# A fused retention-attention and MLP kernel: attention blocks in 64x64 quadrants without the masked quarter, swapped key halves, and a reordered lead-in

## The chip, the cores and the metric

The kernel runs on one core of a Trainium2 chip. The metric is the device time of one execution in microseconds; a kernel's time is the median of its runs. The span in a profile is some 1.8 us shorter than the time of the same execution. Ratios are the mean time of one kernel's fast runs over the mean of the other's fast runs of the same rounds, so not quite the ratio of the quoted medians.

Names used below: PE is TensorE, DVE VectorE, ACT ScalarE, POOL GpSimd, SP SyncE.

## The reference

```python
# q, k, v: (8 batches, 8 heads, 576 positions, 64), float32
scores = (1/8) * q @ k^T
rel    = pos[:, None] - pos[None, :]
ret    = scores * where(rel >= 0, gamma_h ** rel, 0)     # causal, with decay per head
x      = (ret @ v), laid out as (4608 tokens, 512)
h      = x @ w_in                                        # 512 x 2048
out    = (h * sigmoid(1.702 * h)) @ w_out                # 2048 x 512
```

## The kernel before

The tokens are cut into 36 units of 128; four units make a chunk, nine chunks make the run. For each chunk the kernel computes `up` (16 column blocks of 4 matmuls of 128x512, then Gelu on ACT) and `down` (4 row blocks of 16 matmuls). The attention of the next chunk's units is put between them in `block`, two units at a time: `inter` (contribution of the state of earlier units), `scores` (keys times queries of the following two units), a mask product on DVE, `values`. `state` updates a 64x64 key-value state per head. Keys and queries come as float32 over POOL's DMA queue, are cast to bf16 by it, and from unit 8 on are transposed by a DMA transpose from SP into `kqT`; the first eight units are transposed on PE.

```python
def load_kq(u, which, eng="pool"):          # one DMA for k, one for q (two each for a tail unit)
    ... e.dma_start(kqn[sl][p0:p0+n, which, :, :], src[b, :, s0:s0+n, :].rearrange("h p d -> p h d"))

def dma_transpose(u):                       # on SP, in order with the stores
    op("sp", lambda e: e.dma_start_transpose(kqT[u % NQT].ap(), kqn[sl]...), ...)

def scores(u, banks):                       # 8 matmuls in 64x128 shape
    for hp in range(HP):
        for hh in range(2):
            matmul(ps32(banks[hh])[:, P*hp : P*hp+P],
                   qt[64*hh : 64*hh+64, hp, :], qt[64*hh : 64*hh+64, HP+hp, :])

def values(u, slot):                        # 8 matmuls in 128x64 shape
    ... matmul(xbank(hh, slot)[64*pb : 64*pb+64, g, :], vp[u % NVP][:, 2*hp+hh, :], pm[u % 4][hh][:, hp, :])

def block(j):                               # inter is in 64x64 shape
    inter(2*j, 0); inter(2*j+1, 1)
    scores of units 2j+2, 2j+3
    values(2*j, 0); values(2*j+1, 1)
    ...

def lead_in():
    load_kq(0, 0); load_kq(0, 1); load_v(0); iota_small()
    load_v(1, after=["kq0_1"])              # v of units 0 to 3 from SP, each behind a landing
    load(1); iota_large(); load_win(0); ... load(2) ... load(3); weights
    for u in range(4, NLD): load(u)         # NLD = 12
    ... units 0 to 3, half-width ups, full ups, down of chunk 0 with units 4 to 7 ...

def steady():
    for c in range(1, NCH):
        for u in range(4*c+6 if c > 1 else NPE, min(4*c+10, NU)):
            dma_transpose(u)                # chunk 1: units 8 to 13, behind all stores of chunk 0
        for f in range(NF):
            up(c, f)
            if f % 4 == 2: state(m); load(m + NLD)
            ...
            if c == 1 and f == 8: scores(8, "CD"); scores(9, "EX")
```

## Time and profile before

The median on the first chip is 334.57 us (333.93 to 336.38).

| part of the run (PE timeline) | from, us | lasts, us |
|---|---|---|
| chunk 0 and everything ahead of it | 0 | 69.8 |
| chunk 1 | 69.8 | 44.7 |
| chunks 2 to 7, each | 114.5 | 31.1 to 31.6 |
| chunk 8 (no attention) | 303.0 | 30.5 |

From the page of before: the busy share of PE, the granted clock and the DMA in 40 slices of 8.3 us, in tenths, and the chain of waits by engine.

```profile
PE   6365999984499999999999999999999999999996
PEclk9557899998589999999999999999999999999999
DMA  9999999999999199339915992870170162011012
PE 83%; DMA 9%; ACT 3%; DVE 2%; issue 2%; SPq 1%; POOL 0%; POOLq 0%
```

PE is full except in the first four slices, in slices 9 to 11 and at the very end. The waits that the change goes after lie in the first two of these places; elsewhere only PE work can be saved. The second hole is this, in the chain in order of time (start, length, what):

```profile
71.11 1.54 SPq L342
72.76 15.07 DMA kqT<-kqn
```

and from PE's side (start, length, instructions, and in brackets the idle time before and what ended it):

```profile
76.98 1.03 PE L457 MATMUL psA<-xT,w_in_sb 128*128 128x512 bf16 x4
81.88 0.28 PE L404 MATMUL psC<-kqT 64*128 64x128 bf16 x1 [3.88 <-DMA kqT<-kqn]
87.89 0.28 PE L404 MATMUL psE<-kqT 64*128 64x128 bf16 x1 [5.40 <-DMA kqT<-kqn]
88.83 1.49 PE L457 MATMUL psB<-xT,w_in_sb 128*128 128x512 bf16 x3 [0.33 <-issue]
```

The transposes of units 8 and 9 are issued at 71.1 and 72.8 us, and the second lands 15 us after its issue. PE stands for most of 11 us, and its matmuls then run at half clock.

A steady block of two units looks like this in PE's timeline (lines left out between the ends of each group):

```profile
201.57 0.24 PE L392 MATMUL psX<-kqT,kv 64*64 64x128 bf16 x1
...
201.66 0.22 PE L392 MATMUL psY<-kqT,kv 64*64 64x128 bf16 x1
201.80 0.23 PE L404 MATMUL psB<-kqT 64*128 64x128 bf16 x1
...
202.21 0.22 PE L404 MATMUL psE<-kqT 64*128 64x128 bf16 x1
202.35 0.30 PE L423 MATMUL psX<-pm,vp 128*64 128x128 bf16 x4
...
202.71 0.28 PE L423 MATMUL psY<-pm,vp 128*64 128x128 bf16 x4
203.15 0.38 PE L468 MATMUL psA<-w_out_sb,gT 128*128 128x512 bf16 x1 [0.16 <-issue]
```

Starts tell more than lengths here, because matmuls overlap. Pairs of scores start 0.055 us apart; at each change of shape (64*64 to 64*128, to 128*64, to 128*128) the start is some 0.09 us later than that pace would give. One record is missing ahead of the last line, which is why 203.15 is 0.22 us late.

### The profile page before, as it was taken

How to read it: one execution, taken by the hardware profiler on the slowest of the kernel's cores; microseconds unless marked ns; L12 is line 12 of the kernel's file. 1: busy time of each engine (PE TensorE's matmuls, PEld its weight loads, DVE VectorE, ACT ScalarE, POOL GpSimd, SP SyncE). 2: the span in 40 equal slices, each digit the busy share in tenths (PEclk: the TensorE clock that was granted, in tenths of full speed). 3: DMA queues.
4: the chain of work that ended last, by engine and by line, in shares of the span. 5: the costliest groups of instructions: out<-in, count | busy, mean ns of one | idle time of the engine just before them, and what ended most of it. 6: DMA issues, size and time to landing. Idle time of an engine off the chain costs nothing.

```text
span 333.5 us, 5231 instructions
## 1 busy us (share of the span) xinstructions
PE 301.1 (90%) x2198; PEld 144.8 (43%) x2232; DVE 119.3 (36%) x224; ACT 127.9 (38%) x230; POOL 107.3 (32%) x136
## 2 busy tenths in 40 slices
PE   6365999984499999999999999999999999999996
PEld 2133634531154444443544444444445444443344
DVE  4325002861234435433551455324534434510000
ACT  5463653343041263136314611661164136314721
POOL 8996298962160068008303630400000000000000
PEclk9557899998589999999999999999999999999999
DMA  9999999999999199339915992870170162011012
GB/s 99 158 194 202 209 213 224 234 231 135 100 131 202 64 175 177 100 97 166 180 65 130 188 156 65 132 88 34 66 158 2 63 80 47 2 63 63 2 31 94
DMA packets 121063, 40.19 MB, mean 120 GB/s; under 512 B 110160, under 2 KB 114512, under 8 KB 121040
## 3 DMA queue, kind: packets, MB, share of 16 engines
q0 software_dynamic: 81920, 22.03, 63.4%
q1 hardware_dynamic: 39120, 17.83, 28.8%
q8 instruction: 17, 0.28, 0.3%
q14 instruction: 6, 0.05, 0.0%
HBM read 36.70 MB, written 9.44 MB: 138 GB/s over the span
## 4 chain that ended last, share of the span: by engine, by line
PE 83%; DMA 9%; ACT 3%; DVE 2%; issue 2%; SPq 1%; POOL 0%; POOLq 0%
PE psA L468 19%; PE psB L457 18%; PE psA L457 18%; PE psB L468 18%; DMA kqT<-kqn 5%; DMA vn<-in_v_dram 3%; PE psK L353 2%; PE psX L423 2%; DVE pm L412 1%; PE psY L423 1%; PE psX L392 1%; PE psB L404 1%; DMA kqn<-in_q_dram 1%; PE psD L404 1%; ACT kqT L325 1%
## 5 line engine op out<-in xcount | busy, mean ns | idle before, releaser
L457 PE MATMUL psA<-xT,w_in_sb 128*128 128x512 bf16 (+1 forms) x297 | 76.8, 379 | 3.2 <-ACT gT L462 2.8
L457 PE MATMUL psB<-xT,w_in_sb 128*128 128x512 bf16 (+1 forms) x296 | 76.0, 379 | 0.7 <-issue 0.3
L468 PE MATMUL psA<-w_out_sb,gT 128*128 128x512 bf16 (+1 forms) x288 | 66.7, 373 | 2.2 <-issue 2.1
L209 POOL DMA_DIRECT2D kqn<-in_k_dram x40 | 35.5, 899 | 101.5 <-PE psK L353 91.6
L468 PE MATMUL psB<-w_out_sb,gT 128*128 128x512 bf16 (+1 forms) x285 | 63.9, 373 | 0.3 <-issue 0.2
L462 ACT ACTIVATE gT<-psB 128x512 bf16<-128x512 f32 (+1 forms) x76 | 43.7, 574 | 37.4 <-PE psB L457 37.1
L462 ACT ACTIVATE gT<-psA 128x512 bf16<-128x512 f32 (+1 forms) x76 | 43.7, 574 | 21.8 <-PE psA L457 21.7
L366 DVE CAST kv<-psK 64x256 bf16<-64x256 f32 x56 | 23.6, 422 | 77.3 <-PE psK L353 76.9
L457 PEld LDWEIGHTS psA<-xT,w_in_sb 128*128 128x128 bf16 x304 | 27.0, 101 | 41.4 <-ACT gT L462 16.9
L468 PEld LDWEIGHTS psA<-w_out_sb,gT 128*128 128x128 bf16 x304 | 28.2, 98 | 31.4 <-ACT gT L462 1.0
L468 PEld LDWEIGHTS psB<-w_out_sb,gT 128*128 128x128 bf16 x288 | 27.9, 98 | 31.5
L457 PEld LDWEIGHTS psB<-xT,w_in_sb 128*128 128x128 bf16 x304 | 25.9, 101 | 31.5 <-ACT gT L462 10.5
L478 ACT ACTIVATE osb<-psA 128x512 f32<-128x512 f32 x18 | 10.7, 597 | 71.3 <-PE psA L468 71.3
L209 POOL DMA_DIRECT2D kqn<-in_q_dram x40 | 35.3, 889 | 2.6 <-issue 2.6
L222 POOL DMA_DIRECT2D vn<-in_v_dram x36 | 32.4, 909 | 4.6 <-issue 4.5
L307 DVE TENSOR_TENSOR vp<-vn,vfac 128x512 bf16<-128x512 f32 x36 | 24.6, 689 | 15.7 <-DMA vn<-in_v_dram 15.0
L478 ACT ACTIVATE osb<-psB 128x512 f32<-128x512 f32 (+1 forms) x18 | 10.5, 586 | 48.7 <-PE psB L468 48.7
L412 DVE TENSOR_TENSOR pm<-psC,mask 128x512 bf16<-128x512 f32 x20 | 13.7, 683 | 22.0 <-PE psD L404 22.0
L412 DVE TENSOR_TENSOR pm<-psB,mask 128x512 bf16<-128x512 f32 x12 | 8.3, 691 | 36.9 <-PE psB L404 36.9
L404 PE MATMUL psC<-kqT 64*128 64x128 bf16 x88 | 9.3, 230 | 8.1 <-ACT kqT L325 4.2
L423 PE MATMUL psX<-pm,vp 128*64 128x128 bf16 x144 | 10.1, 233 | 5.6 <-DVE pm L412 5.6
L353 PE MATMUL psK<-vp,kqn 128*128 128x128 bf16 x128 | 13.3, 231 | 0.0
(61 smaller groups left out, 195.6 us busy)
## 6 DMA issues: line engine op xcount, KB each, us to landing
out_dram<-osb SPq DMA_DIRECT2D x31, 256.0 KB, 2.1
vn<-in_v_dram POOLq DMA_DIRECT2D x28, 256.0 KB, 12.8
kqn<-in_k_dram POOLq DMA_DIRECT2D x32, 128.0 KB, 11.4
kqn<-in_q_dram POOLq DMA_DIRECT2D x32, 128.0 KB, 11.4
w_in_sb<-in_moe_w_in_dram POOLq DMA_DIRECT2D x8, 256.0 KB, 11.4
w_out_sb<-in_moe_w_out_dram POOLq DMA_DIRECT2D x4, 512.0 KB, 20.5
out_dram<-osb SPq DMA_DIRECT2D x10, 128.0 KB, 2.3
vn<-in_v_dram SPq DMA_DIRECT2D x4, 256.0 KB, 9.5
```

Of the source, the lines that this page charges most:

```text
L209: e.dma_start(kqn[sl][p0 : p0 + n, which, :, :], src[b, :, s0 : s0 + n, :].rearrange("h p d -> p h d"),)
L222: e.dma_start(vn[sl][p0 : p0 + n, :, :], v[b, :, s0 : s0 + n, :].rearrange("h p d -> p h d"),)
L307: op(eng, lambda e: e.tensor_tensor(vp[u % NVP].ap(), vn[sl].ap(), vfac[:, ty, :, None].to_broadcast([P, H, DH]), ALU.mult), reads=[f"vn{s ...
L353: op("pe", lambda e, hp=hp: e.matmul(bank["K"][:, P * hp : P * hp + P], kqn[sl][:, 0, 2 * hp : 2 * hp + 2, :], vp[u % NVP][:, 2 * hp : 2 * ...
L366: op("dve", lambda e, dst=dst, src=src: e.tensor_copy(dst, src), reads=["K"], writes=[f"kv{u % NKV}_{hh}"])
L404: op("pe", lambda e, hp=hp, hh=hh: e.matmul(ps32(banks[hh])[:, P * hp : P * hp + P], qt[64 * hh : 64 * hh + 64, hp, :], qt[64 * hh : 64 * ...
L412: op("dve", lambda e: e.tensor_tensor(pm[u % 4][hh].ap(), ps32(banks[hh]).rearrange("p (a i) -> p a i", i=P), m[:, None, :].to_broadcast([ ...
L423: op("pe", lambda e, g=g, pb=pb, hh=hh, hp=hp, s=s: e.matmul(xbank(hh, slot)[64 * pb : 64 * pb + 64, g, :], vp[u % NVP][:, 2 * hp + hh, :] ...
L457: op("pe", lambda e, a=a: e.matmul(bank[b][:, n0:n1], w_in_sb[:, a, P * f : P * f + P], xT[c % 2][:, a, n0:n1], start=(a == 0), stop=(a == ...
L462: op("act", lambda e: e.activation(gT[c % 2][:, f, n0:n1], bank[b][:, n0:n1], AF.Gelu_apprx_sigmoid), reads=[b], writes=[f"g{c % 2}_{f}_{j ...
L468: op("pe", lambda e, f=f: e.matmul(bank[b][:, 0 : n1 - n0], gT[c % 2][:, f, P * r : P * r + P], w_out_sb[:, f, n0:n1], start=(f == 0), sto ...
L478: op("act", lambda e: e.activation(dst, src, AF.Copy), reads=[b], writes=[f"osb{i}_{n0}"])
```

## The change

It has two intents. First, units 9 to 35 do all their attention in 64x64 shape, so that the shape never changes inside a block, and they don't compute the quarter of key-query pairs in which all keys lie after all queries. Without more, one half of the array would stream 128 columns per head and the other 64. So the loads of the odd heads put keys (and v) into the partitions with their halves of 64 swapped: then each quadrant has a full and a half product in turn. That needs eight DMAs per unit instead of three. The author did not want two row groups to write one PSUM bank at once, so the values come in two phases, and the second waits for the first. Second, the lead-in is reordered: v of units 1 to 3 goes to POOL's queue behind k and q, tables are made by cheaper instructions, units 2 and 3 are interleaved with half-width ups, four banks are used. Units 8 and 9 are transposed behind the second store of chunk 0, and loads from unit 10 on wait for a transpose.

```diff
+def head(u, pb, g, hh):
+    if u < NSW:                        # NSW = 9
+        return 4 * pb + 2 * g + hh
+    return 4 * pb + 2 * hh + g
...
+    todo = [(slice(0, 4), slice(0, H, 2), r) for r in unit_rows(u)]          # load_kq, u >= NSW
+    odd = halves(u, True) if which == 0 else unit_rows(u)
+    todo += [(slice(4, 8), slice(1, H, 2), r) for r in odd]
...
+QR = {(0, 0): (0, 0, P), (0, 1): (64, 128, 64), (1, 0): (64, 0, 64), (1, 1): (0, 64, P)}
...  scores
+for pb in range(2):
+    for g in range(2):
+        for c in (g, 1 - g):
+            q0, o0, n = QR[c, g]
+            for hh in range(2):
+                matmul(ps32(banks[hh])[64*c : 64*c+64, 192*pb+o0 : 192*pb+o0+n],
+                       qt[64*hh : 64*hh+64, 2*g+pb, 64*c : 64*c+64],
+                       qt[64*hh : 64*hh+64, HP+2*g+pb, q0 : q0+n])
...
+def values_half(u, slot, phase, after_ops=()):
+    for g, r in ((0, 0), (0, 1), (1, 1), (1, 0)):
+        hh = r ^ phase ...             # row group r writes bank hh
...  block
+    first = [values_half(u, sl, 0)]    # ahead of the next units' scores
     scores(u, b) ...
+    values_half(u, sl, 1, first)       # behind them
...  lead_in, steady
-load_v(1, after=["kq0_1"])             # on SP
+load(1)                                # k, q, v on POOL
-for u in range(4, NLD): load(u)
+for u in range(4, NPE + 2): load(u)    # to unit 9
+                if r == 1:             # in down of chunk 0
+                    dma_transpose(8)
+                    dma_transpose(9)
+                if c == 1:
+                    for u in range(10, 14):
+                        load(u, after=["T1_0"])          # T1 is unit 9's transpose here
+                for u in range(4 * c + 10, 4 * c + 14):
+                    load(u, after=[f"T{(4 * c + 9) % NQT}_0"])
```

## The prediction

> **What bounds it now.** The chain of waits puts 73% of the span on the dense up and down matmuls. In the timeline a chunk of four units (128 dense 128x512 matmuls and their attention) repeats every 31.4 to 31.5 us from 146 us on; four dense matmuls take 0.86 us, so 27.6 us is dense and 3.8 us attention. PE is full there at clock 1.0, so only PE time counts. The first two differ: chunk 0 ends at 69.8 us and chunk 1 takes 44.8 us.
>
> **Lead-in.** The chain waits 9.3 us for v of unit 1, whose load the sync queue issues only after unit 0's q landed: PE stands from 12.4 to 17.0 us. The change issues it right behind k and q of unit 1. Then the activation engine makes tail tables (1.65 us) and loads its table (1.28 us); units 2 and 3 wait for copies and masks while half-width up matmuls stand at the end. The change interleaves these and uses four banks. I expect down of chunk 0 to start at about 38.5 us, not 48.0. Earlier brings little: v of unit 4 lands at 42.5 us now, and the bytes keep their order. Units 4 to 7 arrive just in time; chunk 1 starts at 60 to 61 us: 9 us gained.
>
> **Chunk 1.** The transposes of units 8 and 9 are issued behind the last store of chunk 0 (71.1 us), collide with loads up to unit 18, and take 15.1 us on the chain. PE stands 77.8 to 88.8 us, then runs at half clock to 94: 13 us lost. The change issues them after the second store and holds loads 10 to 13 until unit 9 is transposed. 13 us gained.
>
> **Quadrants, units 9 to 35.** In a two-unit block the scores now take 0.47 us, values 0.46 us, each change of tile shape about 0.09 us. The Trainium skill (TensorEngine Tiling (Array Packing), Key Properties) says changing the mode drains TensorE; the gaps agree. After: 192 instead of 256 columns per head pair in each quadrant, so about 0.32 us each, and two changes of shape disappear. A full block takes 1.58 us; I estimate 1.1: 0.4 to 0.5 us in each of 13 or 14 blocks, 5.5 us. Inter-chunk 64x64 matmuls of 64 columns already start 8 ns apart, so issue should hold.
>
> **Costs.** A unit's loads become 8 DMAs, not 3. POOL takes 0.88 us for 1024 rows and 0.68 for 512, so an estimated 0.58 for 256: 5 us per unit, 2.65 before; 20 to 22 us of a 31 us chunk. It is tight in chunk 1: unit 13 is transposed at about 81 us, needed at about 84.
>
> **Sum.** 334.6 - 9 - 13 - 5.5 = 307. Predicted 306 us, 300 to 316 in 8 of 10. Faster by over 2%: 0.95; within: 0.04; slower: 0.01.
>
> **Profile signs.** Chunk 1 starts near 60 us and lasts about 31; DMA kqT leaves the chain; steady chunks 30.4 to 30.7 us; a block 1.1 us without gaps between inter, scores and values; POOL above 45% busy.
>
> **What would make it wrong.** Loads 10 to 13, behind the transpose and slower to issue, come late and give back up to 8 us in chunk 1; twice as many small matmuls and weight loads limit issue (a block stays at 1.5); the second values phase's wait on PE itself.

## More of the kernel before

In the stretch from 50 to 90 us the transposes took this long from issue to landing:

```profile
DMA to landing us min/median/max: 10.7/14.5/16.1
```

Taken as start of `inter` to start of `down`, with such records allowed for and the last block, which has no scores, left out, steady blocks last 1.36 to 1.48 us.

## The result and the profile after

The change ran in 309.96 us (309.55 to 310.32, 4 runs) against 334.25 us for before on the same chip (4 runs): ratio 0.9265, 95% interval 0.9218 to 0.9312. The time lies in the predicted range, 4 us above the predicted middle.

| part of the run | before, us | after, us | gained | predicted gain |
|---|---|---|---|---|
| to the start of chunk 1 | 69.8 | 62.0 | 7.8 | 9 |
| chunk 1 | 44.7 | 31.5 | 13.2 | 13, and a little of the blocks |
| chunks 2 to 7 | 188.5 | 184.0 | 4.5 | about 5 of the 5.5 |
| chunk 8 | 30.5 | 30.5 | 0 | 0 |

The same lines of the page of after:

```profile
PE   6779999899999999999999999999999999999996
PEclk9556999999999999999999999999999999999999
DMA  9999999899999969996999699979999760010022
PE 92%; DVE 2%; ACT 2%; DMA 2%; POOL 1%; issue 0%; POOLq 0%
```

The hole of chunk 1 is nearly closed and that of the lead-in is smaller. In chunk 1 the DMA queues now run like this. First SP's transposes of units 8 and 9 (start, length, count), then POOL's first load of unit 10, with POOL's idle time before it:

```profile
53.32 4.30 SPq L419 DMA_TRANSPOSE kqT<-kqn  x2
```

```profile
59.82 2.00 POOL L241 DMA_DIRECT2D kqn<-in_k_dram  x3 [14.78 <-DMA kqT<-kqn]
```

From 50 to 90 us the transposes land after

```profile
DMA to landing us min/median/max: 3.0/4.2/4.9
```

instead of a median of 14.5 us. A steady block in PE's timeline, to be laid beside the one of before:

```profile
200.93 0.24 PE L468 MATMUL psX<-kqT,kv 64*64 64x128 bf16 x1
...
201.18 0.22 PE L536 MATMUL psX<-pm,vp 64*64 64x128 bf16 x1
...
201.35 0.22 PE L495 MATMUL psB<-kqT 64*64 64x128 bf16 x1
...
201.70 0.22 PE L536 MATMUL psY<-pm,vp 64*64 64x128 bf16 x1
...
201.84 0.20 PE L536 MATMUL psY<-pm,vp 64*64 64x64 bf16 x2
201.98 2.76 PE L583 MATMUL psA<-w_out_sb,gT 128*128 128x512 bf16 x12
```

It is all 64*64; scores of two units take 0.35 us from their first start to the next group's, and the only changes of shape left are those at its two ends, from and to 128*128. Steady blocks last 0.94 to 1.09 us, most of them 0.42 us less than before. POOL is busy 61% of the span, 32% before; a unit's loads take it 5.4 us, 2.65 before.

### The profile page after: what moved, and what is told of

It is laid out like the page before. It is cut to its first block, busy times and chain, and to the rows that moved or that the text cites. A ratio compares the mean times of both kernels' runs of the same rounds, so it can differ in the third digit from the quotient of the medians.

```text
span 308.0 us, 6292 instructions
## 1 busy us (share of the span) xinstructions
PE 296.5 (96%) x2664; PEld 142.1 (46%) x2664; DVE 118.0 (38%) x246; ACT 126.2 (41%) x238; POOL 187.3 (61%) x276
## 4 chain that ended last, share of the span: by engine, by line
PE 92%; DVE 2%; ACT 2%; DMA 2%; POOL 1%; issue 0%; POOLq 0%
PE psA L583 21%; PE psB L572 20%; PE psA L572 20%; PE psB L583 19%; PE psK L430 3%; PE psX L468 2%; DMA kqn<-in_q_dram 2%; ACT kqT L402 1%; POOL kqn L241 1%; PE psY L536 1%; PE psC L484 1%; DVE pm L503 1%; PE psX L536 1%; PE psX L523 1%; PE psE L392 1%; PE psD L495 1%
## 5 line engine op out<-in xcount | busy, mean ns | idle before, releaser
L241 POOL DMA_DIRECT2D kqn<-in_k_dram x94 | 68.3, 807 | 52.5 <-DMA kqT<-kqn 49.5
L572 PE MATMUL psB<-xT,w_in_sb 128*128 128x512 bf16 (+1 forms) x296 | 74.8, 376 | 2.2 <-ACT kqT L402 2.2
L572 PE MATMUL psA<-xT,w_in_sb 128*128 128x512 bf16 (+1 forms) x296 | 74.9, 377 | 0.1
L259 POOL DMA_DIRECT2D vn<-in_v_dram x93 | 68.9, 854 | 3.2 <-issue 3.2
L583 PE MATMUL psA<-w_out_sb,gT 128*128 128x512 bf16 (+1 forms) x304 | 69.9, 374 | 0.0
L241 POOL DMA_DIRECT2D kqn<-in_q_dram x70 | 57.0, 892 | 0.0
L583 PEld LDWEIGHTS psB<-w_out_sb,gT 128*128 128x128 bf16 x288 | 27.9, 98 | 31.5
L572 PEld LDWEIGHTS psB<-xT,w_in_sb 128*128 128x128 bf16 x296 | 24.7, 99 | 32.7 <-ACT gT L577 10.5
L593 ACT ACTIVATE osb<-psB 128x512 f32<-128x512 f32 (+1 forms) x18 | 10.5, 586 | 48.7 <-PE psB L583 48.7
L511 DVE TENSOR_TENSOR pm<-psB,maskp 128x384 bf16<-128x384 f32 x12 | 6.7, 558 | 38.3 <-PE psB L495 38.3
L384 DVE TENSOR_TENSOR vp<-vn,vfac_s 128x512 bf16<-128x512 f32 x27 | 18.5, 689 | 1.1 <-DMA vn<-in_v_dram 0.6
L430 PEld LDWEIGHTS psK<-vp,kqn 128*128 128x128 bf16 x128 | 9.7, 102 | 6.9 <-issue 0.7
L595 DVE COPY osb<-psA 128x256 f32<-128x256 f32 x1 | 0.4, 425 | 32.5 <-PE psA L583 32.5
L560 DVE TENSOR_TENSOR xT<-psX,gq 128x512 bf16<-128x512 f32 x13 | 8.9, 682 | 5.2 <-PE psX L536 5.2
```

The costliest lines, as they stand in the source:

```text
L241: e.dma_start(kqn[sl][p0 : p0 + n, which, ds, :], src[b, ss, s0 : s0 + n, :].rearrange("h p d -> p h d"),)
L259: e.dma_start(vn[sl][p0 : p0 + n, ss, :], v[b, ss, s0 : s0 + n, :].rearrange("h p d -> p h d"),)
L384: op(eng, lambda e: e.tensor_tensor(vp[u % NVP].ap(), vn[sl].ap(), (vfac if u < NSW else vfac_s)[:, ty, :, None].to_broadcast([P, H, DH]), ...
L430: op("pe", lambda e, hp=hp: e.matmul(bank["K"][:, P * hp : P * hp + P], kq_pair(u, 0, hp), v_pair(u, hp), start=(c == 0 and hp == 0), stop ...
L511: op("dve", lambda e: e.tensor_tensor(pm[u % 4][hh][:, 0:384].rearrange("p (a i) -> p a i", i=192), ps32(banks[hh])[:, 0:384].rearrange("p ...
L560: op("dve", lambda e: e.tensor_tensor(xT[ch % 2][:, x_tiles(u0, hh), P * jj : P * jj + 2 * P].rearrange("p g (u t) -> p u g t", u=2), ps32 ...
```

## The experiments

All twelve ran correctly. Runs of one table row share their chip's runs of before; chips differ, so a row's ratio is safer than its median. "Chunk 1" is the time from its first up matmul to that of chunk 2, and "block" the steady block, both from the profiled execution. The medians are those of the fast runs; one of four runs was slow in e2 (324.47 us) and in e4 (440.01 us).

| run | median, us | ratio to before | chunk 1 starts | chunk 1 lasts | block |
|---|---|---|---|---|---|
| the change | 309.96 | 0.927 | 62.0 | 31.5 | 0.94 to 1.09 |
| e1 lead-in only | 320.38 | 0.957 | 62.3 | 36.3 | 1.36 to 1.48 |
| e2 quadrants only | 322.23 | 0.959 | 69.7 | 32.5 | 0.94 to 1.09 |
| e5 quadrants, nothing skipped | 319.14 | 0.954 | 60.9 | 42.7 | 1.13 to 1.26 |
| e6 skipped, not swapped | 317.44 | 0.946 | 61.1 | 37.9 | 1.13 to 1.25 |
| e7 phases adjacent | 313.04 | 0.935 | 60.7 | 32.9 | 1.21 to 1.37 |
| e3 late transposes | 315.56 | 0.944 | 60.5 | 38.5 | 0.94 to 1.09 |
| e4 no gate | 318.04 | 0.949 | (profile slow) | | |
| e8 before, loads in pieces | 328.12 | 0.980 | 69.8 | 37.0 | 1.36 to 1.48 |
| e9 lead-in only, loads in pieces | 315.25 | 0.942 | 61.9 | 32.0 | 1.36 to 1.48 |
| e10 early table | 310.04 | 0.927 | 61.2 | 33.5 | 0.94 to 1.09 |
| e11 warm and table | 309.79 | 0.926 | 60.6 | 33.0 | 0.94 to 1.09 |
| e12 early transposes | 308.86 | 0.924 | 59.5 | 33.2 | 0.94 to 1.09 |

The first question is whether the two halves of the change give what the prediction gave them.

### e1: the lead-in without the quadrants

```diff
-NPE, NSW = 8, 9
+NPE, NSW = 8, 36
```

> The change's new lead-in and load order, but every unit keeps the old tile shapes and the old three loads per unit. Theory (lead-in and chunk 1 give about 18 of the 24 us, quadrants about 5.5): 315.5 us, blocks of 1.5 to 1.6 us, steady chunks 31.4 us. Rival (quadrants give nothing, all is lead-in): 310 us.

It took 320.38 us, 5 us more than the theory and 10 more than the rival. The blocks are the old ones and steady chunks last 31.35 to 31.55 us, as the theory said. But chunk 1 took 36.3 us: PE stands again for a DMA transpose, now that of unit 11.

```profile
81.52 0.23 PE L484 MATMUL psD<-kqT 64*128 64x128 bf16 x1 [2.46 <-DMA kqT<-kqn]
```

The reordered lead-in does not remove the stall by itself. That was not in the prediction.

### e2: the quadrants without the lead-in

Lead-in, tables and the order of loads, transposes and stores are those of before; blocks and loads from unit 9 on are those of the change.

```diff
-lead_in(), steady(): as in the change
+lead_in(), steady(): as before (transposes of 8 to 13 at the start of chunk 1, nothing gated)
+    setup_iota_s(); setup_vfac_s(); setup_maskp()    # in free places of the lead-in
```

> The old lead-in and load order with the new quadrant blocks and swapped loads from unit 9 on. Theory (the parts add): 334.3 - 5.5 = 329 us. Rival (the eight loads per unit cost more in the old order, because POOL issues units 9 to 11 for about 5 us each before the transposes of 8 and 9 can run freely): 332 us or more, with a longer stall in chunk 1.

Both expectations were wrong: the fast runs took 318.5, 322.2 and 322.9 us, at the median 12.8 us less than before. The blocks give their 5 us, and the rest is chunk 1, which lasts 32.5 us in the profile although its transposes are issued at 71 us as before. (The profile is of the fastest run, so in the other runs chunk 1 was probably longer.) So most of the stall of before goes away with nothing moved. What differs in the loads is that POOL takes 5.4 us per unit: it has just got to unit 14 when the transposes come, where before it was done with unit 18.

That gave a new theory. It is the backlog in the DMA queues that delays the transposes, and cutting each unit's loads into eight pieces paces POOL so that no backlog forms. The prediction had entered the eight pieces as a cost that hides. Two runs test this alone.

### e8: the kernel before, with only its loads cut into pieces

```diff
+def pieces(u, cut):
+    rows = unit_rows(u)
+    if u < 9: return [(slice(None), r) for r in rows]
+    half = [(p0 + i, 64, b, s0 + i) for p0, n, b, s0 in rows for i in range(0, n, 64)]
+    return [(slice(0, H, 2), r) for r in rows] + [(slice(1, H, 2), r) for r in (half if cut else rows)]
```

> The kernel before, with one edit: from unit 9 on the loads of a unit are cut into the same eight pieces as in the change, with nothing swapped and the old tile shapes, lead-in and order. Theory (the eight pieces pace POOL to some 5.4 us per unit, so no backlog stands in the DMA queues when the transposes of 8 and 9 come): chunk 1 takes 33 to 34 us instead of 44.8, about 324 us. Rival (the short stall of quadrants_only came from its shorter blocks or another part): 334 us or more, chunk 1 above 42 us.

It took 328.12 us, 6.5 us less than before, and chunk 1 lasted 37.0 us. (The ratio's interval, 0.975 to 0.984, spans the 2% line, so the verdict is unclear at 2%, but the gain itself is clear of noise.) That is between the two, and closer to the theory: the pieces alone remove 7.7 us of chunk 1, with nothing else changed. PE still waits once, for unit 9:

```profile
81.58 0.28 PE L415 MATMUL psE<-kqT 64*128 64x128 bf16 x1 [3.32 <-DMA kqT<-kqn]
```

The transposes of 50 to 90 us land after

```profile
DMA to landing us min/median/max: 6.3/9.9/11.3
```

so they are faster than before but not quick. (In e8 as in before SP issues all six in a row, so they may also hold up one another; no run tests that.) The backlog itself can be counted, from issues and landings in the traces: when the transposes of units 8 to 11 were issued, 1.2 to 2.1 MB of loads were issued and not landed in before, and 0.2 to 0.5 MB in e8. The 4.5 us between e8 and e2 in chunk 1 are probably in the main the choice of run: e2's profile is of its fastest run, 3.7 us ahead of its next one. By the medians of fast runs e2 is 5.9 us faster than e8, and the blocks give about 5 of these.

### e9: the lead-in without the quadrants, loads in pieces

The edit is that of e8, made to e1.

> As lead_in_only (old tile shapes throughout), but with the loads from unit 9 on cut into the eight pieces, unswapped. Theory (without the pieces loads 10 to 13 flood the queues and delay the transposes of 10 and 11; with them the flood is paced): chunk 1 takes 32 to 32.5 us instead of 36.3, total 315 to 316 us. Rival (the stall of lead_in_only has another cause): 320 us.

The theory held: 315.25 us, chunk 1 32.0 us, and no wait for a transpose. e1 and e9 differ in nothing but the cutting of the loads, and the cutting is worth 5.1 us. The landing times of 50 to 90 us in e1 and then in e9:

```profile
DMA to landing us min/median/max: 3.1/5.8/12.3
```

```profile
DMA to landing us min/median/max: 3.0/4.0/5.8
```

The slow ones are gone. In e1 POOL issues loads 10 to 13 in 10.5 us, from 60.1 to 70.7, and the transposes of 10 and 11 come into their midst. In e9 the same four take over 20 us. When the transposes of 10 and 11 were issued, 0.9 and 1.0 MB of loads were in flight in e1, and 0.4 and 0.3 MB in e9. The Trainium skill (DMA: Bandwidth & Descriptors, Issuing engines are not separate DMA queues) says that DMAs of all engines run on the same 16 DMA engines and interleave; these landing times agree, with a median of 4.0 us at a paced load stream and up to 12.3 us at a flooded one. The pieces are also smaller DMAs, and no run has small DMAs at the old pace or large ones slowed down; so that the pace and not the size does it is argued from the bytes in flight (and e4 below), not shown by a run of its own.

### e3: the transposes of 8 and 9 late, as before

```diff
-                if r == 1:
-                    dma_transpose(8)
-                    dma_transpose(9)
+                # at the start of chunk 1, behind the last store of chunk 0
```

> The change, but the DMA transposes of units 8 and 9 are issued behind the last store of chunk 0, as before; loads 10 to 13 still wait for unit 9's transpose. Theory (the late issue is the cause): with the queues quiet the transposes take 4 to 5 us each and unit 9 is there at about 68.5 us, in time for its scores at 70.2; but loads 10 to 13 start 8 to 9 us later, so blocks of chunk 1 wait: about 318 us. Rival (only contention with loads mattered): 310 us.

It took 315.56 us, 2.4 us under the theory's figure and 5.6 over the rival's. POOL takes up loads 10 at 66.68 us instead of 59.82, 6.9 us later, and chunk 1 lasts 38.5 us instead of 31.5, 7.0 us longer (it also starts 1.5 us earlier, so the run as a whole loses 5.6 us):

```profile
66.68 2.00 POOL L241 DMA_DIRECT2D kqn<-in_k_dram  x3 [22.11 <-DMA kqT<-kqn]
```

So the early issue is worth having, but by a longer way than the prediction said: it does not spare the wait for 8 and 9 (they were in time here too) but lets the loads of 10 to 13 start.

### e4: no gate on loads 10 to 13

```diff
-                    for u in range(10, 14): load(u, after=["T1_0"])    # in chunk 1
+            for u in range(10, 14): load(u)                            # in the lead-in
```

> The change, but loads 10 to 13 are issued at once in the lead-in instead of waiting for unit 9's transpose. Theory (issuing the transposes early is enough): they collide with the loads and take up to 15 us, unit 9 comes at about 68 us, still before its scores at 70.2: 310 to 312 us. Rival (the gate is needed): unit 9 comes after 72 us, PE stands and cools, 315 us or more.

The theory fell: the three fast runs took 317.5 to 318.2 us, so the gate is worth 8 us. The profiled run fell in a slow state (440.01 us at a mean clock of 0.652), and the fast runs left no trace here. Where the 8 us lie is therefore not shown; that they are a late transpose is my guess from e1 and e8. The slow trace is a hint of the same: in it the transposes of units 8 and 9 take 11.2 and 15.1 us from issue to landing, with 1.2 and 1.0 MB of loads in flight, although these loads are in pieces. Small pieces alone thus did not keep the transposes quick there.

The next three look into the block.

### e5: quadrants, nothing skipped, nothing swapped

```diff
-NPE, NSW = 8, 9
+NPE, NSW, NQ = 8, 36, 9       # old head order and loads; blocks from unit 9 on in 64x64
+for hp in range(HP):
+    for c in range(2):
+        q0 = 0
+        for hh in range(2):
+            matmul(ps32(banks[hh])[64*c : 64*c+64, P*hp+q0 : P*hp+P],
+                   qt[64*hh : 64*hh+64, hp, 64*c : 64*c+64], qt[64*hh : 64*hh+64, HP+hp, q0:P])
```

> All attention of units 9 to 35 in 64x64 quadrants, but nothing skipped and no heads swapped, three loads per unit. Theory (about half of the gain of a block is the two changes of shape, half the columns): about 313 us, blocks near 1.3 us. Rival 1 (only the shape changes matter): 310. Rival 2 (only the skipped columns matter): 315.5.

The total can't be used: without the pieces, chunk 1 stalls as in e1, and longer (42.7 us in the profiled run, which was the slowest of the four). The blocks can: the shortest take 1.13 us, where before has 1.36 and the change 0.94. So keeping one shape is worth 0.23 us of a block (net of what twice the matmuls and the two phases of values, which come with it, cost or save) and the skipped columns 0.19 us. The Trainium skill (TensorEngine Tiling (Array Packing), Key Properties) says that changing the tiling mode drains TensorE; this agrees, at 0.23 us for the two changes that go, or some 0.11 us each; the starts in the block of before gave some 0.09 us.

### e6: skipped, but not swapped

```diff
-        q0 = 0
+        q0 = 64 * c                # and 64 * r in the values
```

> As quadrants_full, but the masked quarter is skipped without swapping the key halves of odd heads, so that one half of the quadrants still streams 128 columns per head and the other 64. Theory (the fuller quadrants set the time, so the swap is what makes the skip pay): the same as quadrants_full, about 313 us. Rival (the number of columns counts, not their balance): about 310 us.

Its blocks last 1.13 to 1.25 us, the same as e5's within 0.01 us, with a quarter fewer columns. The first line of a block of two units and the first of the `down` behind it, in e5 (212.12 to 213.59) and e6 (207.49 to 208.95), both 0.22 us late for a missing record as above:

```profile
212.12 0.24 PE L468 MATMUL psX<-kqT,kv 64*64 64x128 bf16 x1
213.59 0.59 PE L584 MATMUL psA<-w_out_sb,gT 128*128 128x512 bf16 x2 [0.16 <-issue]
```

```profile
207.49 0.24 PE L468 MATMUL psX<-kqT,kv 64*64 64x128 bf16 x1
208.95 0.59 PE L584 MATMUL psA<-w_out_sb,gT 128*128 128x512 bf16 x2 [0.16 <-issue]
```

The theory held for the blocks: where one half of the quadrants streams 128 columns a head and the other 64, the fuller half sets the time, and only the swap turns the skipped quarter into time. The total (317.44 us) again carries a stalled chunk 1.

### e7: the two phases of the values back to back

```diff
     first = [values_half(u, sl, 0)]
-    scores(u, b) of the next units
     values_half(u, sl, 1, first)
+    scores(u, b) of the next units
```

> The change, but the second phase of the values, which waits on PE for the first, follows it directly instead of after the next units' scores. Theory (the wait for the first phase to drain is hidden by the scores): exposed it costs 0.2 to 0.25 us in each of 13 blocks, about 313 us. Rival (the wait costs nothing): 310 us.

The theory held: 313.04 us, blocks 1.21 to 1.37 us, some 0.27 us more than in the change. From the list of waits (who waited for whom, us in total, times, longest), of e7 and then of the change:

```profile
PEld psY L536 <- PE psX L536: 2.8, 13, 0.2
```

```profile
PEld psY L536 <- PE psX L536: 0.2, 1, 0.2
```

The one left in the change is the last block, which has no scores to put between. The reason for the phases is a rule that I took from the Trainium skill (TensorEngine Tiling (Array Packing), Gotcha 1: PSUM Pressure): different row tiles can't access one PSUM bank at once. No run here breaks it, so what would happen is not shown.

### e10, e11 and e12: attempts at a faster version

The change's lead-in ends 1 to 2 us later than predicted, and PE ran at half clock in it in the profile. e10 loads the Gelu table earlier. e11 also fills PE's gaps with idle matmuls.

```diff
+op("act", lambda e: e.activation(junk.ap(), lnsc.ap(), AF.Gelu_apprx_sigmoid))   # e10, behind the last Exp
+fill(n, b)                                                # e11: n matmuls of zeros into a free bank
```

> The change, with one tiny Gelu on a 128x1 tile right after the last exponential, so that the activation table is loaded while the engine is idle at 12 us and not on the chain at 15.4 us. Theory: 1.3 us earlier in the lead-in, 308.5 us. Rival (the lead-in is held by the arrival of loads): 310 us.

> As early_table, and TensorE's gaps from 5 to 22 us are filled with idle matmuls into free banks, so that the granted clock is not halved from 9 to 28 us. Theory (the lead-in of the change is bound there by cold matmuls on the chain): down of chunk 0 starts at about 36 us instead of 40.1, chunk 1 at 58 to 59, total 306 us. Rival (DMA binds: units 4 to 7 do not land earlier): chunk 1 starts at 61 to 62 us as before, 309 to 310 us.

Neither gained: 310.04 and 309.79 us. Chunk 1 starts at 61.2 and 60.6 us, but the seven kernels with this lead-in (the change, e1, e3, e5, e6, e7 and e9) start it between 60.5 and 62.3 us in their profiles, so that is no gain to speak of. And chunk 1 became longer by at least as much as it started earlier, because PE now waits for the transpose of unit 13, for 1.77 us in e10 and 1.23 us in e11:

```profile
87.06 0.24 PE L496 MATMUL psD<-kqT 64*64 64x128 bf16 x1 [1.23 <-DMA kqT<-kqn]
```

e12 tries to start loads 10 to 13 earlier by putting the transposes of 8 and 9 behind the first store of chunk 0. It also moves the table load, the fills and unit 1's product.

```diff
-                if r == 1:
+                if r == 0:
                     dma_transpose(8)
                     dma_transpose(9)
```

> A version meant to beat both: the transposes of units 8 and 9 are issued behind the first store of chunk 0 instead of the second, which lets loads 10 to 13 start earlier; the activation table is loaded after the first state copy, unit 1's mask products go before its table product, and fewer idle matmuls fill TensorE's gaps. Theory (early_table and warm_and_table gave their gain of 0.8 to 1.4 us back in chunk 1 because loads 10 to 13 start only after unit 9's transpose): POOL takes up loads 10 at 53 to 55 us instead of 59.8, no wait for the transpose of unit 13 is left, chunk 1 lasts 31.5 us and starts at 59 to 60.6, total 306.5 to 308.5 us. Rival (the time from chunk 1's start is pinned by something else): 309.5 to 310 us.

The step that mattered failed. The transposes were issued no earlier (53.57 us; 53.32 in the change) and POOL took up loads 10 at 59.58 us (59.82 in the change); PE still waits 1.28 us for the transpose of unit 13. From SP's list of waits between 40 and 70 us in e12:

```profile
SPq L116 <- DMA kqn<-in_q_dram: 18.2, 3, 11.2
```

SP waits 11.2 us at one time for keys and queries to land. So it is not the store that holds the transposes but the arrival of units 8 and 9, which stand in the queue behind the weights and units 0 to 7. The clock from 10 to 28 us was 1.00 instead of 0.50, from the windows of the change and then of e12 (PE, PEld, DVE, ACT and POOL busy; clock; DMA, summed over packets that overlap, so that it can pass 1; GB/s):

```profile
10.00:28.00 18.00, 14.88 (x136) 8.96 (x136) 10.37 (x21) 9.03 (x26) 18.00 (x24) 0.50 1.41 189
```

```profile
10.00:28.00 18.00, 13.07 (x155) 7.98 (x156) 12.30 (x27) 11.18 (x32) 18.00 (x24) 1.00 1.43 189
```

The fills need not be the reason, and the clock is not what makes the lead-in late. e1, with the change's lead-in and no fill, had 1.00 in the same stretch (e9 too; the change had 0.50, the others without fill 0.56 to 0.69):

```profile
10.00:28.00 18.00, 13.79 (x133) 8.24 (x130) 9.76 (x18) 8.62 (x25) 18.00 (x24) 1.00 1.42 186
```

Yet `down` of chunk 0 starts at 40.4 us in e1 and 40.0 in e9, no earlier than the 40.1 of the change at half clock. And three of the change's four runs had a mean clock of 1.00 and took 309.55 to 310.32 us, the profiled one, at 0.967, 309.82.

In e12 `down` of chunk 0 starts at 37.6 us (38.6 to 40.4 in all kernels with the change's lead-in) and chunk 1 at 59.5; which of its edits did that is not shown. The total is 308.86 us (307.95 to 311.24, 6 runs), between the theory's and the rival's figures, ratio 0.924, interval 0.921 to 0.927. The intervals of the change and of e12 overlap, and they ran on different chips: that e12 beats the change is not shown.

What pins the end of chunk 1 is seen best across kernels. The time from POOL's first load of unit 10 to the start of chunk 2 is 33.7 us in the change (59.8 to 93.5), 32.8 in e7 and e11, 33.1 in e10 and e12, and 32.3 in e3, wherever chunk 1 starts. In the change itself PE doesn't wait, but the transpose of unit 13 (issued at 83.61 us) lands at 86.66, and PE reaches that unit's scores at 87.02: the slack is under 0.4 us.

```profile
83.61 1.23 SPq L419 DMA_TRANSPOSE kqT<-kqn  x1
```

```profile
87.02 0.22 PE L495 MATMUL psD<-kqT 64*64 64x128 bf16 x1
```

## Why the prediction was right, and where it was not

- **The total** was in the range: 309.96 us for a predicted 306 (300 to 316).
- **Chunk 1, 13 us: right in size, incomplete in cause.** The measured 13.2 us (and a little of the blocks in it) match. The prediction gave them to the early issue of the transposes and the gate. The runs show three parts, each needed: e3 without the early issue loses 7.0 us of chunk 1 and 5.6 in all; e4 without the gate loses 8 us in all; and e1, without the eight pieces, loses 4.8 us of chunk 1, of which e9 gets back 4.2 by adding only them. In the old order the pieces alone remove more than half of the stall (e8). That the size came out right is thus in part luck: the pieces were put in for the swap, and the prediction counted them as a cost only.
- **The step that failed** is "A unit's loads become 8 DMAs, not 3 ... 20 to 22 us of a 31 us chunk", entered under costs. POOL's time was right (5.4 us a unit, 5 predicted), its sign was not: cutting the loads gained 5.1 us (e9 against e1), most likely because the slower issue keeps the DMA queues short when transposes come.
- **"It is tight in chunk 1"** was right: unit 13's transpose was predicted at about 81 us and needed at about 84; it was there at 86.7 and needed at 87.0. It cost nothing in the change, and it is what took back the gains of e10, e11 and, in part, e12.
- **Lead-in, 9 us: mis-sized; it gave 7.8.** `down` of chunk 0 starts at 40.1 us, not 38.5. The half clock from 10 to 28 us is not the reason (e1 and e9 at full clock: 40.4 and 40.0). The same lead-in reached 38.6 us in e3, so part of this is spread from run to run. A better lead-in did not shorten the run, because chunk 1's end is pinned by the loads.
- **Quadrants, 5.5 us: right in mechanism and nearly in size.** e9 differs from the change only in the blocks and the swap, and takes 5.3 us more (315.25 against 309.96 us, on two chips). A block lost 0.42 us (0.4 to 0.5 predicted), about half by the shapes and half by the columns, and chunks 2 to 7 lost 4.5 us together; chunk 1 has the rest. The last block gained nothing, having no scores.
- **The wait for the first phase**, feared under "what would make it wrong", is hidden by the scores between (e7: 0.27 us a block when it is not). Issue did not limit the doubled number of matmuls.
- **The parts do not add.** e1 gains 14.6 us and e2 12.8, together 27; the whole gains 24.3, as both cure the same stall in part.

Left open: where e4's 8 us lie; whether the pieces help by their pace alone; and which part of the reordered lead-in (the place of the v loads, the tables, the interleaving, the banks) gives how much of its 7.8 us, since no run takes them apart.

## What to carry to other kernels

A backlog of loads can delay another DMA that is on the critical path. With no other transpose in flight, the DMA transposes here landed after 3.0 to 6.3 us behind at most 0.7 MB of loads, and after 6.9 to 12.3 us behind 0.9 to 2.1 MB. Where that happens, pacing the loads (by smaller pieces, or by a wait on a landing) can be worth more than speeding them up. When packing small matmuls into quadrants, check that every quadrant skips the same amount (in e6, where they did not, skipping gained nothing); here it also paid to keep one tile shape through a block. Before improving a stage, look for what pins the end of the next one: here three altered lead-ins moved the start of chunk 1 and hardly its end.

## What the Trainium skill lacked or had wrong

- DMA: Bandwidth & Descriptors, Issuing engines are not separate DMA queues: it says that the queues interleave, but not what a backlog does to a DMA transpose. Between 50 and 90 us the median landing time was 14.5 us behind a load backlog, and 4.0 to 4.2 us with the same loads in eight pieces and behind a gate.
- DMA: Bandwidth & Descriptors has nothing on the use of pieces to pace POOL. Cutting a unit's three loads into eight took POOL from 2.65 to 5.4 us a unit and made the kernel before 6.5 us faster (e8).
- TensorEngine Tiling (Array Packing), Key Properties: it says that a change of mode drains TensorE, without a figure. Here a change cost some 0.11 us (the two that go, 0.23 us of a block, e5), or 0.09 us by the starts in the block of before.
- TensorEngine Tiling (Array Packing): it does not say that the columns must be balanced over the quadrants. With a quarter of them skipped unevenly, a block took as long as with none skipped (1.13 us and up, e5 and e6).
